# New engine orders, found over several draws of the transposes' landing times, in a linear-attention and gated-MLP block

## The chip, the cores and the metric

The kernel runs on one core of a Trainium2 chip. A core has TensorE (PE) for matmuls, VectorE (DVE), ScalarE (ACT) and GpSimd (POOL) for elementwise work, and SyncE (SP), which here only issues DMAs. Each engine works through its own instructions in order and waits on semaphores for the others. The metric is the device time of one execution in microseconds; the time of a kernel is the median of its runs.

## The reference

One pre-normalised transformer block on x of 2048 tokens by 448 features, in bfloat16: linear attention with 16 heads of 28, then a gated MLP of width 1792, each with a residual.

```python
def _A_ref(x, wqkv, wo):
    B, S, D = x.shape
    H = 16; Dh = D // H
    qkv = (x @ wqkv).reshape(B, S, 3, H, Dh).transpose(2, 0, 3, 1, 4)
    q, k, v = qkv[0], qkv[1], qkv[2]
    phi = lambda t: jnp.where(t > 0, t + 1, jnp.exp(t)) + 1e-6
    pq, pk = phi(q), phi(k)
    kv = jnp.einsum("bhsd,bhse->bhde", pk, v)
    z = jnp.einsum("bhsd->bhd", pk)
    num = jnp.einsum("bhqd,bhde->bhqe", pq, kv)
    den = jnp.einsum("bhqd,bhd->bhq", pq, z)[..., None] + 1e-6
    o = num / den
    return o.transpose(0, 2, 1, 3).reshape(B, S, D) @ wo

h  = x + _A_ref(layernorm(x), wqkv, wo)
h2 = h + (gelu(layernorm(h) @ w_gate) * (layernorm(h) @ w_up)) @ w_down
```

## The kernel before

The 2048 tokens are 16 tiles of 128. The work is a graph of 878 named tasks, and a task is one instruction, one DMA or, on TensorE, a group of matmuls. The number in a name is the tile, or for q the chunk, or for the MLP the block. Each engine has its own written list of task names in ORDERS, and place() puts the tasks of the engine into that order. finalize() and emit() then make semaphores and waits from the dependences: a task waits for the tasks on other engines that wrote what it reads, or still read what it writes. So the lists alone set what stands behind what on an engine, and they can add waits but no wrong result.

The first part goes over all tiles. VectorE takes the statistics (bnst, bnag, lines 462 and 463), ScalarE makes 1/sqrt of the variance (ln, rstd), VectorE or, from tile 4 on, GpSimd normalises (norm, lines 486 and 487). The normalised tile must be turned so that features lie on partitions: tiles 0 to 3 by TensorE (tr, and ev copies the result on ScalarE), the others by a transposing DMA that SyncE issues (xT, line 526), for which ScalarE first doubles the last 64 columns (dup). TensorE then makes k and v of a tile (k, v), ScalarE takes exp (ek) and copies v (evv), GpSimd clamps (cl, line 566), VectorE finishes phi(k) (ph, line 568), and TensorE sums phi(k) times v over the tiles (acc, two halves a and b). In between come the q chunks (qa, qb; eq and rq on ScalarE, cq and pq on GpSimd or VectorE, lines 618, 619 and 627). kz1 and kz2 take the masked sum to SBUF.

The second part goes over pairs of tiles. TensorE makes numerator and denominator (nd, halves a and b), VectorE divides (rd, om, lines 654 and 655), a transposing DMA turns the result (oT, line 729), TensorE multiplies by wo (wo, halves a and b), VectorE adds the residual and takes statistics (hr, line 660; hbnst, hbnag), GpSimd makes 1/sqrt and normalises (hnegm line 481, vpe line 474, pow line 476, normh line 487), VectorE copies the tile to a second place (wrap, line 749), and a transposing DMA turns it (hT, line 750). Tiles 0 and 1 use TensorE for both turns instead (tro, trh; evo, evh).

The MLP goes over chunks of 2, 2, 4, 4 and 4 tiles. A block gu holds the gate and the up product for one slice of the width (28 matmuls of 256 columns in the first two chunks, 14 of 512 after them), ScalarE takes gelu in two halves (ge, line 830), VectorE multiplies (hm, line 832), and down adds up the product with w_down for a pair of tiles (halves a and b) or, for the last four, a tile; out adds the residual (line 756) and dout writes the tile to HBM (line 757).

TensorE's matmuls contract over 64 rows, so one stream works on rows 0 to 63 and one on rows 64 to 127, and they take turns in the program (both()). A half a writes bank P from the first rows and bank Q from the second, its half b the other way round, so b waits for the end of a. PSUM has 8 banks; a gu block uses two of them, and takes the pair that the block two before it used. Almost every matmul comes from line 430 of one helper, the last four down tasks from line 780.

SyncE issues in the order of the fifth list, and each transposing DMA holds it for over a microsecond.

Of the kernel before, what the change touches and what calls it, by code (L numbers as in the profile page):

```python
# [11 lines left out]


ORDERS = (
    "warm0 warm1 tr0 tr1 k0 v0 k1 tr2 v1 tr3 k2 k3 v2 v3 acc0a qa00 acc0b acc1b qb00 k4 acc1a acc2a v4 k5 acc2b acc3b"
    " v5 k6 qa01 v6 qb01 k7 acc3a acc4a v7 acc4b acc5b k8 acc5a acc6a v8 k9 k10 v9 v10 qa10 acc6b acc7b qb10 acc7a k11"
    " acc8a k12 v11 v12 k13 acc8b acc9b v13 acc9a acc10a k14 k15 v14 acc10b acc11b v15 acc11a acc12a acc12b acc13b"
    " qa20 acc13a acc14a qb20 acc14b acc15b acc15a qa11 nd1 nd0 qb11 qa30 nd2a tro1 nd2b qb30 qa21 tro0 qb21 wo1 wo0"
    " qa31 wo2a qb31 wo2b trh0 trh1 nd4a nd4b gu1 gu0 gu3 gu2 wo4a gu5 wo4b gu4 gu7 nd6a nd6b gu6 down0a gu8 wo6a gu9"
    " wo6b down0b nd8a gu11 nd8b gu10 gu13 gu12 down2a wo8a down2b wo8b gu15 nd10a gu14 nd10b gu17 gu16 gu19 gu18 gu21"  # L20
    " wo10a wo10b gu20 nd12a gu23 nd12b gu22 gu25 gu24 gu27 gu26 wo12a down4a wo12b gu28 nd14a gu29 nd14b down4b gu31"
    " gu30 gu33 wo14a gu32 wo14b gu35 gu34 down6a gu36 gu37 down6b gu39 gu38 gu41 gu40 gu43 gu42 gu45 gu44 gu47 gu46"
    " gu49 gu48 gu51 gu50 down8a gu53 down8b gu52 down10a gu55 down10b gu54 down12 down13 down14 down15 down15b",
    "dwk dwv dwk_t tbl ln0 rstd0 ln1 rstd1 ev0 ev1 ln2 ln3 rstd2 rstd3 ek0 evv0 ln4 ev2 rstd4 ev3 ek1 dup4 evv1 dup5"
    " ln6 rstd6 ek2 evv2 evv3 ek3 dup6 dup7 ln8 rstd8 eq0 eq1 dup9 ln12 ek4 rstd12 evv4 ln10 rstd10 ek5 dup8 evv5"
    " dup10 ln14 rstd14 ek6 eq3 evv6 eq2 dup12 dup11 ek7 evv7 ek8 evv8 dup14 dup13 ek9 dup15 evv9 ek10 evv10 eq4 eq5"
    " ek11 evv11 ek12 evv12 evv13 ek13 ek14 evv14 evv15 ek15 eq8 rq8 eq6 rq6 evo1 eq12 evo0 rq10 eq10 rq12 hln1 hrstd1"
    " hln0 hrstd0 eq14 evh0 tbl2 rq14 ge1_0 ge1_1 ge0_1 ge0_0 ge3_1 ge3_0 ge2_1 ge2_0 ge5_1 ge5_0 ge4_1 ge4_0 ge7_1"
    " ge7_0 ge6_0 ge6_1 ge8_0 ge8_1 ge9_1 ge9_0 ge11_1 ge11_0 ge10_0 ge10_1 ge13_1 ge13_0 ge12_0 ge12_1 ge15_0 ge15_1"
    " ge14_0 ge14_1 ge17_0 ge17_1 ge16_0 ge16_1 ge19_0 ge19_1 ge18_0 ge18_1 ge21_0 ge21_1 ge20_0 ge20_1 ge23_1 ge23_0"  # L30
    " ge22_1 ge22_0 ge25_1 ge25_0 ge24_1 ge24_0 ge27_1 ge27_0 ge26_1 ge26_0 ge28_0 ge28_1 ge29_1 ge29_0 ge31_0 ge31_1"
    " ge30_1 ge30_0 ge33_1 ge33_0 ge32_0 ge32_1 ge35_0 ge34_1 ge34_0 ge35_1 ge36_0 ge36_1 ge37_0 ge37_1 ge39_1 ge39_0"
    " ge38_1 ge38_0 ge41_1 ge41_0 ge40_0 ge40_1 ge43_0 ge43_1 ge42_1 ge42_0 ge45_1 ge45_0 ge44_0 ge44_1 ge47_0 ge47_1"
    " ge46_1 ge46_0 ge49_0 ge49_1 ge48_0 ge48_1 ge51_0 ge51_1 ge50_0 ge50_1 ge53_1 ge53_0 ge52_1 ge52_0 ge55_1 ge55_0"
    " ge54_1 ge54_0",
    "wqz pkones bnst0 bnag0 bnst1 bnag1 norm0 v1ones norm1 bnst3 bnst2 bnag3 bnag2 bnst4 bnst5 norm2 bnag4 bnag5"
    " norm3 bnst7 ph0 bnst9 bnst6 bnag7 bnag6 bnst12 ph1 bnst8 bnst11 bnag8 bnag9 ph2 bnst13 bnst10 ph3 bnag13 bnag12"
    " bnag10 bnag11 pq0 pq1 ph4 bnst14 bnst15 bnag14 bnag15 ph5 ph6 pq3 pq2 ph7 ph8 ph9 ph10 pq4 pq5 ph11 ph12 ph13"
    " ph14 ph15 kz2 kz1 rd1 rd0 om1 om0 cq6 rd2 om2 rd3 om3 cq8 pq6 hr1 hbnst1 hr0 hbnag1 hbnst0 hbnag0 normh1 wrap1"
    " normh0 wrap0 hr2 hr3 evh1 hbnst2 rd4 rd5 om4 hbnag2 hbnst3 om5 hm1_0 hm1_1 hbnag3 cq12 cq10 hm0_1 hm0_0 pq10"  # L40
    " cq14 wrap2 pq8 hm3_0 hm3_1 wrap3 pq12 pq14 hm2_1 hm2_0 hm5_1 hr5 hm5_0 hbnst5 hr4 hm4_1 hbnst4 hm4_0 hbnag5"
    " hbnag4 rd6 om6 rd7 om7 hm7_0 hm7_1 hm6_0 wrap4 wrap5 hm6_1 hm8_0 hm8_1 hr6 hm9_0 hbnst6 hm9_1 hr7 hbnag6 hbnst7"
    " hbnag7 out0 out1 rd9 rd8 hm11_1 hm11_0 om8 wrap7 hm10_0 hm10_1 om9 wrap6 hm13_1 hm13_0 hm12_0 hm12_1 out2 hr8"
    " hr9 hbnst8 hbnst9 hm15_1 hm15_0 out3 hbnag8 hbnag9 rd10 hm14_1 hm14_0 rd11 om10 hm17_0 hm17_1 om11 wrap8 wrap9"
    " hm16_0 hm16_1 hm19_0 hm19_1 hm18_0 hm18_1 hm21_0 hm21_1 hr11 hr10 hbnst10 hbnst11 hbnag10 hbnag11 hm20_0 hm20_1"
    " rd13 hm23_1 hm23_0 rd12 om13 hm22_1 hm22_0 om12 wrap10 wrap11 hm25_1 hm25_0 hm24_1 hm24_0 hm27_0 hm26_1 hm27_1"
    " hm26_0 hr12 hr13 hbnst12 hbnst13 hm28_0 hm28_1 hbnag12 hbnag13 rd15 rd14 om15 hm29_1 hm29_0 wrap12 om14 wrap13"
# [865 lines left out]
```

## Time and profile before

| | us |
|---|---|
| median of 3 runs | 198.86 (198.32 to 199.07) |
| the profiled execution | 198.63 |
| its span, first to last instruction | 196.9 |

| engine | busy us | share | instructions |
|---|---|---|---|
| TensorE matmul | 190.9 | 97% | 2192 |
| VectorE | 117.3 | 60% | 301 |
| ScalarE | 78.8 | 40% | 205 |
| GpSimd | 43.4 | 22% | 90 |

A group or timeline row gives the line, the engine, the operation, what it writes and reads, the shape and the count. In a timeline the first two numbers are start and length in microseconds, and a bracket names the idle time before it and what ended it. Two matmul streams run side by side and matmuls overlap their neighbours, so a task's cost is its start to the next task's start, not its length. The chain of waits is followed back from the last instruction: at each step to what released it.

### The profile page before, as it was taken

To read this page: it belongs to the slowest core of one execution; us is meant where nothing else is said; L and a number is where in the kernel's file an instruction comes from. 1 tells how busy PE (TensorE), PEld (TensorE's weight loads), DVE (VectorE), ACT (ScalarE), POOL (GpSimd) and SP (SyncE) were. 2 spreads that over 40 slices of the span, in tenths; PEclk is the share of its full clock that TensorE was granted. 3 is DMA by queue.
4 is the path that set the end of the run, shared out by engine and by line. 5 is a ranking of instruction groups with operands and counts; after the bars stand their busy time and mean duration, and the time that the engine had idled before them with its cause. 6 is when DMAs were issued, how large, how long until landed. Compare 5 with 4: busy or idle time off the path is not lost.

```text
span 196.9 us, 5339 instructions
## 1 busy us (share of the span) xinstructions
PE 190.9 (97%) x2192; PEld 131.2 (67%) x2192; DVE 117.3 (60%) x301; ACT 78.8 (40%) x205; POOL 43.4 (22%) x90
## 2 busy tenths in 40 slices
PE   7899999999899999999999999999999999999994
PEld 7455656553497888998764689955555566777554
DVE  3999636357698955852967845846545554240612
ACT  3799876579672412220342441142214444211100
POOL 3189984300015040500320400500500000000000
DMA  6943466999933243153152160290550000010111
GB/s 195 374 108 70 82 108 156 260 244 214 341 66 63 41 82 68 47 91 62 50 100 50 27 125 0 48 126 23 30 88 27 3 0 0 3 47 3 47 47 47
DMA packets 37256, 17.53 MB, mean 89 GB/s; under 512 B 28272, under 2 KB 36336, under 8 KB 37232
## 3 DMA queue, kind: packets, MB, share of 16 engines
q1 hardware_dynamic: 36352, 16.45, 38.3%
q10 hardware_dynamic: 880, 0.75, 1.2%
q8 instruction: 17, 0.28, 0.6%
q14 instruction: 7, 0.06, 0.1%
HBM read 8.72 MB, written 1.84 MB: 54 GB/s over the span
## 4 chain that ended last, share of the span: by engine, by line
PE 83%; DVE 8%; DMA 4%; POOL 2%; issue 1%; ACT 0%; SPq 0%; DVEq 0%; POOLq 0%
PE ps L430 76%; PE ps L780 5%; DMA oT<-o_sb 2%; DVE st L462 2%; DVE x_sb L660 2%; DMA x_sb<-in_A_x_dram 2%; DVE hh L832 1%; POOL hn L487 1%; DVE o_sb L655 1%; POOL rs L476 1%; DVE x_sb L756 1%; PE ps L495 0%; POOL nm L481 0%; DVE mv L463 0%; DVE pqT L619 0%
## 5 line engine op out<-in xcount | busy, mean ns | idle before, releaser
L430 PE MATMUL ps<-hnT,wgu_sb 64*128 64x512 bf16 (+1 forms) x980 | 90.6, 333 | 0.1
L430 PEld LDWEIGHTS ps<-hnT,wgu_sb 64*128 64x128 bf16 x980 | 61.4, 94 | 22.8 <-DVE hh L832 2.5
L830 ACT ACTIVATE gl<-ps 128x256 bf16<-128x256 f32 x112 | 37.0, 381 | 90.8 <-PE ps L430 74.5
L832 DVE TENSOR_TENSOR hh<-ps,gl 128x256 bf16<-128x256 f32 x112 | 42.5, 418 | 31.5 <-ACT gl L830 31.0
L430 PE MATMUL ps<-wd_sb,hh 64*128 64x448 bf16 x336 | 34.4, 349 | 0.0
L430 PEld LDWEIGHTS ps<-wd_sb,hh 64*128 64x128 bf16 x336 | 25.1, 94 | 6.6 <-DVE x_sb L756 0.2
L430 PE MATMUL ps<-wkv_sb,xnT 64*128 64x448 bf16 x192 | 23.1, 350 | 0.1
L756 DVE TENSOR_TENSOR x_sb<-ps,x_sb 128x448 bf16<-128x448 f32 (+1 forms) x17 | 9.7, 592 | 20.0 <-PE ps L430 13.0
L462 DVE BATCH_NORM_STATS2 st<-x_sb 128x6 f32<-128x448 bf16 x32 | 18.9, 615 | 2.6 <-DMA x_sb<-in_A_x_dram 2.5
L568 DVE SCALAR_TENSOR_TENSOR pk<-ps,tm 128x448 bf16<-128x448 f32 x16 | 9.9, 621 | 9.3 <-POOL tm L566 5.3
L430 PE MATMUL ps<-xnT,wq_sb 64*128 64x512 bf16 x112 | 15.3, 377 | 0.2 <-ACT pqT L616 0.2
L430 PE MATMUL ps<-wo_sb,oT 64*128 64x448 bf16 x98 | 13.2, 349 | 1.0 <-DVE st L462 0.4
L481 POOL TENSOR_SCALAR nm<-mv 128x2 f32<-128x2 f32 x13 | 3.4, 258 | 48.8 <-DVE mv L463 48.4
L430 PEld LDWEIGHTS ps<-wkv_sb,xnT 64*128 64x128 bf16 x192 | 9.0, 94 | 7.5 <-PE ps L430 0.5
L660 DVE TENSOR_TENSOR x_sb<-ps,x_sb 128x448 bf16<-128x448 f32 x16 | 9.5, 617 | 6.5 <-PE ps L430 5.6
L487 POOL TENSOR_SCALAR hn<-x_sb,nm,rs 128x448 bf16<-128x448 bf16 x14 | 11.0, 792 | 0.8 <-POOL rs L476 0.2
L780 PE MATMUL ps<-wd_sb,hh 128*128 128x448 bf16 (+1 forms) x70 | 10.8, 315 | 0.0
L565 ACT ACTIVATE e<-ps 128x448 bf16<-128x448 f32 x16 | 8.7, 545 | 4.5 <-PE ps L430 3.2
L474 POOL TENSOR_SCALAR ln<-mv 128x2 f32<-128x2 f32 x7 | 1.5, 221 | 39.9 <-DVE mv L463 39.7
L566 POOL TENSOR_SCALAR tm<-e 128x448 bf16<-128x448 bf16 x16 | 9.0, 562 | 5.5 <-ACT e L565 5.4
L430 PEld LDWEIGHTS ps<-wo_sb,oT 64*128 64x128 bf16 x98 | 6.6, 94 | 4.9 <-PE ps L430 1.3
L655 DVE TENSOR_TENSOR o_sb<-ps,rd 128x448 bf16<-128x448 f32 x16 | 9.6, 607 | 0.1
(69 smaller groups left out, 145.2 us busy)
## 6 DMA issues: line engine op xcount, KB each, us to landing
out_dram<-x_sb SPq DMA_DIRECT2D x15, 112.0 KB, 1.7
wgu_sb<-in_B_w_gate_dram SPq DMA_DIRECT2D x7, 224.0 KB, 6.7
wgu_sb<-in_B_w_up_dram SPq DMA_DIRECT2D x7, 224.0 KB, 7.3
wd_sb<-in_B_w_down_dram SPq DMA_DIRECT2D x1, 1568.0 KB, 7.2
x_sb<-in_A_x_dram SPq DMA_DIRECT2D x2, 448.0 KB, 5.4
wkv_sb<-in_A_wqkv_dram ACTq DMA_DIRECT2D x2, 336.0 KB, 3.8
x_sb<-in_A_x_dram SPq DMA_DIRECT2D x3, 224.0 KB, 4.4
wo_sb<-in_A_wo_dram SPq DMA_DIRECT2D x2, 336.0 KB, 4.2
```

The source lines that it names most:

```text
L430: ins = e.matmul(o_, l_, r_, start=s_, stop=p_, **kw)
L462: op("dve", lambda e: e.bn_stats(st[:, t, :], src_ap), [b_src], [b_st[t]], "%sbnst%d" % ("" if mv is mv1 else "h", t), 0.53, key, after=after)
L487: return lambda e: e.tensor_scalar(dst, src[:, t, :], nm[:, t:t + 1], rs[:, t:t + 1], ALU.add, ALU.mult)
L565: act_exp(lambda e: e.activation(e1[:, ie, :], oK, AF.Exp), bank(bk), [b_e1[ie]], "ek%d" % t, _c_act(D), kk)
L566: op("pool", lambda e: e.tensor_scalar(tm1[:, ie, :], e1[:, ie, :], 1.0 + EPS, 0.0, ALU.min, ALU.max), [b_e1[ie]], [b_tm1[ie]], "cl%d" % t ...
L568: op("dve", lambda e: e.scalar_tensor_tensor(pk[:, i, :, 0:GW], psK3, EPS, tm1[:, ie, :].rearrange("p (g e) -> p g e", g=NG), ALU.max, ALU ...
L655: op("dve", lambda e: e.tensor_tensor(o_sb[:, so, oc:oc + D].rearrange("p (a e) -> p a e", e=28), nd3[:, :, 0:28], rd[:, i, :].unsqueeze(2 ...
L660: op("dve", lambda e: e.tensor_tensor(h_sb[:, u, :], ps[:, b, 0:D], x_sb[:, u, :], ALU.add), bank(b) + [b_x[u]], [b_h[u]], "hr%d" % u, 0.5 ...
L756: op("dve", lambda e: e.tensor_tensor(x_sb[:, t, c0:c1], ps[:, bk, c0:c1], h_sb[:, t, c0:c1], ALU.add), bank(bk) + [b_h[t]], [bo], "out%d% ...
L780: ins = e.matmul(ps[:, bk, c0:c1], hh[:, j, hsl(t)], wd_sb[:, j, c0:c1], start=(j == 0), stop=(j == NJ - 1))
L830: G.add("act", lambda e, gi=gi, cs_=cs_, psG=psG: e.activation(gl[:, gi, cs_], psG[:, cs_], AF.Gelu_apprx_tanh), r=bank(BK_G[i]), w=[b_glh ...
L832: op("dve", lambda e, dst=dst, srcU=srcU, srcL=srcL: e.tensor_tensor(dst, srcU, srcL, ALU.mult), bank(BK_U[i]) + [b_glh], [b_ar[j_][t % HR ...
```

## The change

Only the five strings of ORDERS are replaced; no task, size or buffer changes. The lists of before came from a search in which every transposing DMA takes one fixed time from issue to landing; the new ones come from a search that scores an order over several draws of these times. 44 of TensorE's 195 places hold another task, 119 of ScalarE's 208, 213 of VectorE's 301, 48 of GpSimd's 86 and 20 of SyncE's 88; most of these by one to three places. The core of it:

```diff
 # TensorE
-warm0 warm1 tr0 tr1 k0 v0 k1 tr2 v1 tr3 k2 k3 v2 v3 acc0a qa00
+warm1 warm0 tr0 tr1 k0 v0 k1 tr2 tr3 v1 k2 acc0a k3 v2 v3 qa00
...
-acc7a k11 acc8a k12 v11 v12 k13 acc8b acc9b v13 acc9a acc10a k14 k15
+acc7a acc8a k11 k12 v11 v12 k13 acc8b acc9b v13 k14 acc9a k15 acc10a
...
-qa11 nd1 nd0 qb11 qa30 nd2a tro1 nd2b qb30 qa21 tro0 qb21 wo1 wo0 qa31 wo2a qb31 wo2b trh0 trh1 nd4a nd4b
+qa11 nd0 nd1 qb11 qa30 nd2a tro0 nd2b qb30 qa21 tro1 qb21 wo1 wo0 qa31 wo2a qb31 wo2b trh1 trh0 nd4a nd4b
-gu1 gu0 gu3 gu2 wo4a gu5 wo4b gu4 gu7 nd6a nd6b gu6 down0a gu8 wo6a gu9
+gu1 gu0 gu3 gu2 gu5 wo4a wo4b gu4 nd6a gu7 nd6b gu6 down0a gu9 wo6a gu8
...
-wo12b gu28 nd14a gu29 nd14b down4b gu31 gu30 gu33 wo14a gu32 wo14b gu35 gu34 down6a gu36 gu37 down6b gu39
+wo12b gu29 nd14a gu28 nd14b gu31 down4b gu30 gu33 gu32 wo14a gu35 wo14b gu34 gu37 gu36 down6a gu39 gu38 gu41 down6b
...
-gu49 gu48 gu51 gu50 down8a gu53 down8b gu52 down10a
+gu49 gu48 down8a gu50 gu51 gu52 down8b gu53 down10a
 # ScalarE
-ln6 rstd6 ek2 evv2 evv3 ek3 dup6 dup7 ln8 rstd8 eq0 eq1 dup9 ln12 ek4 rstd12 evv4 ln10 rstd10 ek5 dup8
+ln6 dup5 rstd6 evv1 ek2 dup6 ln8 ek3 rstd8 evv2 evv3 dup7 eq1 dup8 eq0 dup9 ln12 ek4 ln10 rstd10 rstd12
...
-eq14 evh0 tbl2 rq14 ge1_0 ge1_1
+eq14 evh0 tbl2 ge1_0 ge1_1 rq14
 # VectorE
-kz2 kz1 rd1 rd0 om1 om0 cq6 rd2 om2 rd3 om3 cq8 pq6 hr1
+kz1 kz2 cq8 rd0 rd1 om0 om1 rd2 om2 rd3 cq6 om3 pq8 pq6 cq12 hr1
...
-hr2 hr3 evh1 hbnst2 rd4 rd5 om4 hbnag2 hbnst3 om5 hm1_0 hm1_1 hbnag3 cq12 cq10 hm0_1 hm0_0 pq10 cq14 wrap2 pq8 hm3_0 hm3_1 wrap3 pq12 pq14
+hr2 hr3 evh1 cq14 hbnst2 rd4 hbnst3 rd5 hbnag2 hbnag3 om5 hm1_0 hm1_1 om4 hm0_1 hm0_0 wrap3 wrap2 pq12 hm3_1 hm3_0 pq14 pq10
...
-rd10 hm14_1 hm14_0 rd11 om10 hm17_0 hm17_1 om11
+rd11 rd10 hm14_0 hm14_1 om11 om10 hm17_1 hm17_0
...
-hm28_0 hm28_1 hbnag12 hbnag13 rd15 rd14 om15 hm29_1 hm29_0 wrap12 om14 wrap13 out5 out4 hm31_0 hm31_1 hm30_1 hm30_0
+hm29_0 hbnag13 hm29_1 hbnag12 rd15 rd14 hm28_0 hm28_1 om15 om14 hm31_0 hm31_1 wrap12 out5 wrap13 out4 hm30_0 hm30_1
 # GpSimd
-negm6 norm6 cl2 norm7 negm8 cl3 norm9 cq0 cq1 negm10 cl4 negm12 norm8 norm10 cl5 norm12 norm11 cl6
+negm6 cl1 norm6 norm7 negm8 cl2 cl3 norm8 norm9 cq1 cq0 negm10 negm12 cl4 norm10 norm11 cl5 norm13 norm12 cl6
...
-cl7 norm13 norm14 cl8 norm15 mask_c powwarm cl9
+cl7 norm14 opad2 norm15 cl8 powwarm cl9
 # SyncE
-oT2 oT3 dwd oT4 oT5 hT2 hT3 oT6 oT7 hT5 hT4 dout0 dout1 oT8 oT9 hT7 hT6 dout2 dout3 oT10 oT11 hT8 hT9 oT13 oT12 hT10 hT11
+oT2 oT3 dwd oT5 oT4 hT3 hT2 oT6 oT7 hT5 hT4 dout1 dout0 oT9 oT8 hT6 hT7 dout2 oT11 oT10 hT9 dout3 hT8 oT13 oT12 hT10 hT11
-oT15 hT12 oT14 hT13 dout5 dout4 hT15 hT14
+oT15 oT14 hT12 dout5 hT13 dout4 hT14 hT15
```

90 rows, old and new, of the table ORDERS are left out of this document.

## The prediction

> **What bounds the kernel now.** I read the page first, then the chain of work that ended last, then TensorE's timeline, then VectorE, GpSimd and the DMAs where TensorE stood. On the page, the busy line, the chain's shares and the DMA queues:
>
> ```profile
> PE 190.9 (97%) x2192; PEld 131.2 (67%) x2192; DVE 117.3 (60%) x301; ACT 78.8 (40%) x205; POOL 43.4 (22%) x90
> q8 instruction: 17, 0.28, 0.6%
> PE 83%; DVE 8%; DMA 4%; POOL 2%; issue 1%; ACT 0%; SPq 0%; DVEq 0%; POOLq 0%
> ```
>
> TensorE bounds it: 97% busy, 83% of the chain. The change leaves all 2192 matmuls in the program, so only time can go in which TensorE stands. The chain in order of time names the places (start, length, what):
>
> ```profile
> 59.80 0.96 POOL hn L487
> ...
> 127.61 3.76 DMA oT<-o_sb
> ```
>
> Near 60 the end hung on GpSimd's norm of h, at 127.6 on a transpose of o_sb that was 3.76 us in flight. TensorE's timeline at these places (start, length, out<-in, matmuls):
>
> ```profile
> 54.81 6.30 PE L430 MATMUL ps<-hnT,wgu_sb 64*128 64x256 bf16 x112
> 60.92 1.40 PE L430 MATMUL ps<-wo_sb,oT 64*128 64x448 bf16 x8
> ...
> 68.20 1.74 PE L430 MATMUL ps<-hnT,wgu_sb 64*128 64x256 bf16 x28
> ```
> ```profile
> 126.31 4.85 PE L430 MATMUL ps<-hnT,wgu_sb 64*128 64x512 bf16 x42
> 131.50 0.93 PE L430 MATMUL ps<-wo_sb,oT 64*128 64x448 bf16 x8 [0.34 <-DMA oT<-o_sb]
> 132.26 1.69 PE L430 MATMUL ps<-hnT,wgu_sb 64*128 64x512 bf16 x14
> 133.77 0.75 PE L430 MATMUL ps<-wo_sb,oT 64*128 64x448 bf16 x6
> ```
>
> Lengths overlap, so work is counted from start to start. Four gate/up blocks take 60.92 - 54.81 = 6.11, or 1.53 each; in the later chunks one takes 133.77 - 132.26 = 1.51. So the three blocks from 126.31 should end at 130.84, and wo14a (the 8 matmuls at 131.50) stood 0.66.
>
> **Part 1: gu5, wo4, nd6 (PE order).** From wo4a (60.92) to gu6 (68.20) 7.28 us go by, with three blocks (gu5, gu4, gu7), wo4a, wo4b, nd6a and nd6b in them. The change makes "wo4a gu5 wo4b gu4 gu7 nd6a nd6b" into "gu5 wo4a wo4b gu4 nd6a gu7 nd6b". A b half writes the banks of its a half from the other rows and waits for its end; side by side they pay that. Prices of both forms:
>
> ```profile
> 103.54 1.89 PE L430 MATMUL ps<-wo_sb,oT 64*128 64x448 bf16 x14
> 105.27 1.67 PE L430 MATMUL ps<-hnT,wgu_sb 64*128 64x512 bf16 x14
> ```
> ```profile
> 79.41 0.37 PE L430 MATMUL ps<-kvz,pqT 64*128 64x116 bf16 x7
> 79.61 0.27 PE L430 MATMUL ps<-hnT,wgu_sb 64*128 64x256 bf16 x1
> ```
>
> wo10a and wo10b side by side take 105.27 - 103.54 = 1.73; an nd half with a block behind it 0.20. New sum: 3 x 1.53 + 1.73 + 2 x 0.20 = 6.72, against 7.28: 0.56 less, if nothing new waits. What could wait is gu5, which writes the banks that hm3 reads. VectorE and GpSimd there:
>
> ```profile
> 54.01 0.61 DVE L709 COPY hnT<-ps 128x896 bf16<-128x896 bf16 x1
> 54.54 0.62 DVE L462 BATCH_NORM_STATS2 st<-x_sb 128x6 f32<-128x448 bf16 x1
> ...
> 56.49 0.61 DVE L655 TENSOR_TENSOR o_sb<-ps,rd 128x448 bf16<-128x448 f32 x1
> 57.07 0.76 DVE L832 TENSOR_TENSOR hh<-ps,gl 128x256 bf16<-128x256 f32 x2
> 57.74 0.17 DVE L463 BATCH_NORM_AGGREGATE mv<-st 128x2 f32<-128x6 f32 x1
> ...
> 59.23 0.68 DVE L619 TENSOR_TENSOR pqT<-xn,pqT 112x1024 bf16<-112x1024 bf16 x1
> ```
> ```profile
> 59.80 2.29 POOL L487 TENSOR_SCALAR hn<-x_sb,nm,rs 128x448 bf16<-128x448 bf16 x2
> 68.43 0.22 POOL L474 TENSOR_SCALAR ln<-mv 128x2 f32<-128x2 f32 x1 [6.34 <-DVE mv L463]
> ...
> 69.81 1.42 POOL L487 TENSOR_SCALAR hn<-x_sb,nm,rs 128x448 bf16<-128x448 bf16 x2 [0.18 <-POOL rs L476]
> ```
>
> In VectorE's new order hbnag3 stands ahead of om5, hm1 and om4. After evh1 (54.01) come cq14, two statistics, two short reciprocals and two aggregates, each some 0.08 shorter than its row by overlap; from these rows I work out that hbnag3 ends at 56.5, not 57.91. From the aggregate to the first norm GpSimd takes 69.81 - 68.43 = 1.38, and the two norms take 1.42, or 2.29 where pqT work of VectorE ran beside them. The new order has none of that work beside them, so 56.6 + 1.38 + 1.42 = 59.4 for both. Then wrap3, wrap2, pq12 (0.68) and the two hm3 (0.76) follow: hm3 ends at about 61.0. gu5 comes up at 60.92, and one late stream of a pair is made up within a matmul: 0.1. om4, moved behind hm1 (57.07 + 0.76) with its 0.61, ends at 58.4, so oT4, then the later of the two transposes, lands at 60.9 with the median of 2.5 us that the next part quotes; wo4a now comes up at 62.5 and has room for 4.1. **I take -0.46**; ends: -0.56, and +2.9 if the norms end where they did (62.09; rival 1).
>
> **Part 2: oT14 ahead of hT12 (SP order), and wo14a one block later (PE order).** SyncE's issues there (the length is SyncE's own), the landings of all 14 transposes of o_sb, and the instruction queue in the stretch of 128 to 130 us:
>
> ```profile
> 126.28 1.23 SPq L750 DMA_TRANSPOSE hnT<-hn  x1
> 127.61 2.35 SPq L729 DMA_TRANSPOSE oT<-o_sb  x1
> ```
> ```profile
> DMA to landing us min/median/max: 2.4/2.5/5.1
> ```
> ```profile
> q8 instruction: 1, 0.02, 4.0%
> ```
>
> oT14 was issued at 127.61, behind hT12's issue of 126.28, held SyncE for 2.35 and landed after 3.76 where the median is 2.5. A 16 KB instruction fetch (0.28 MB / 17) fell into that stretch. With hT12 behind it oT14 is issued near 127 (om14 now follows om15 at once, hm28 ahead of both) and lands at 129.5 to 130.8; wo14a comes up at 130.84 + 1.51 = 132.35. Even 5.1 us would land at 132.1. The stall of 0.66 is gone and gu32 fills the place: **-0.66**. Late next is hm30, which gu32 needs: down4b starts a block later, and on VectorE wrap12, out5, wrap13 and out4 stand ahead of hm30, two of them of om's size (0.61) waiting for down4b. From its end two outs, a wrap and hm30 (0.76) take some 2.3, while gu30 and gu33 take 3.0 on TensorE: 0 to +0.2, taken as 0. hT12 and hT13 feed the last chunk, 20 us later.
>
> [...]
>
> **Part 3: the first 40 us.** More norms stand ahead of the clamps on GpSimd, and opad2 ahead of norm15; VectorE's statistics and ACT's copies are shuffled; the two warm-ups are swapped.
>
> ```profile
> 16.00 1.31 PE L430 MATMUL ps<-wkv_sb,xnT 64*128 64x448 bf16 x12
> ...
> 17.33 0.37 PE L430 MATMUL ps<-v,pk 64*128 64x113 bf16 x8
> ```
> ```profile
> 24.01 1.31 PE L430 MATMUL ps<-wkv_sb,xnT 64*128 64x448 bf16 x12
> ...
> 25.58 0.74 PE L430 MATMUL ps<-wkv_sb,xnT 64*128 64x448 bf16 x6
> ```
>
> v8 and k9 took 1.57 where v4 and k5 took 1.33: 0.24 of waiting for xT10. dup8 moves up nine places on ScalarE, so xT8 to xT10 are issued earlier and this goes. Against it, cl2 stands behind one more norm (0.71, half of the 1.42 above), part of which the earlier rstd6 gives back: I estimate 0.25 for ph2, ph3 and k5. The two cancel and I take 0; ends -0.3 (all of the gap, a little more) and +0.5 (most of a norm).
>
> **The rest.** On SP, pairs swap (oT5/oT4, hT3/hT2, oT9/oT8, hT6/hT7, oT11/oT10), dout3 is issued between hT9 and hT8, dout5 and dout4 around hT13; what comes later by an issue of about 1.2 (126.28 above) is read by all of a pair's readers together or a chunk later: 0. om11 ahead of hm17 makes gu19's second stream late by part of an om (0.61): 0 to +0.2, taken +0.1. trh1 ahead of trh0 uses up the slack of evh0 before gu1: 0 to +0.2, taken 0. Splitting "down6a gu36 gu37 down6b" and "down8a gu53" otherwise puts covered blocks between covered blocks, and swaps within a pair (ge, hm, out, dout) move 0.3 inside slack: 0.
>
> **Sum**, against the profiled execution's 198.63 (span 196.9 and 1.73 around it): -0.46 - 0.66 + 0 + 0.1 = -1.0, so 197.6. The median of the runs, 198.86, is 0.23 above that execution; I forecast 197.8 for the new median, 0.5% less, which is about what a measurement of this kernel can tell from no change.
>
> **Rivals.** 1, slower: with wo4a behind it gu5 loses its cover. If GpSimd's norms end at 62.09 as now, wrap, pq12 and hm3 end near 63.9 and TensorE stands 2.9 at gu5 instead of 0.1: about 200.6. It loses from a norm end of 60.4 on. For it: this chain is in the chain of waits now. Against: the 1.4 us by which hbnag3 moves up, and no pqT work beside the norms. 2, no change: late landings are luck, and one falls elsewhere; the 0.66 is not gained in the median: 198.5. For it: landings run from 2.4 to 5.1; against: the fetch comes by instruction count, and the profiled execution is no slower than the others. 3, no change: the early chain (ph2 to ph5, then cl8 behind norm15) keeps the 0.5 of part 3's upper end or two norms' 1.0: 198.3 to 198.8. For it: each clamp now waits behind norms; against: xT10's gap takes it up. 4, more: part 3 gains its 0.3 too: 197.5.
>
> **How the numbers follow.** Forecast 0.46, of which 0.10 falls just short of 0.5%; rival 1 0.16; rival 2 0.18; rival 3 0.14; rival 4 0.06. Faster 0.36 + 0.06 = 0.42, same 0.10 + 0.18 + 0.14 = 0.42, slower 0.16. The forecast's own range is 197.3 to 198.3, its sum with the small ends. The whole range runs from 197.1 (part 3's gain and the good ends too) to 199.3, which takes in rivals 2 and 3 with a run above the median; beyond it lie rival 1 and little else.
>
> **What would show it.** After: wo14a with no DMA named before it; from the first block after nd4 to gu6 0.4 to 0.5 shorter; the norms at 1.4 for two and ended by 59.5; k10 without its gap. Wrong: hm3 past 61.2, or TensorE behind by over 0.3 at the first product with kvz.

## The result, and the profile after

The changed kernel takes 196.57 us (median of 5 runs, 196.28 to 196.70), where the kernel before took 198.44 in 5 runs beside it: a ratio of 0.9896, interval 0.9876 to 0.9916. The forecast was 197.8; the sign was right and the gain was twice the size. The profiled execution took 196.70 (before 198.63) with a span of 194.9 (before 196.9). From the page of the changed kernel, its busy line and the chain's shares:

```profile
PE 190.3 (98%) x2192; PEld 137.9 (71%) x2192; DVE 116.3 (60%) x301; ACT 78.2 (40%) x205; POOL 42.0 (22%) x90
PE 96%; issue 1%; ACT 1%; DVE 1%; POOL 0%; DVEq 0%; ACTq 0%; POOLq 0%
```

TensorE's share of the chain went from 83% to 96%, and the DMAs with their 4% are gone from it: the transpose of 3.76 us, and the first load of x of 3.26, in whose place this chain runs through TensorE's warm-up. I put the start of each TensorE task beside its start in the profile before (after minus before, in us):

| task | what lies ahead of it | difference |
|---|---|---|
| k0 | warm-up, first statistics | +0.52 |
| qa11 | all k, v and acc | +0.29 |
| qa31 | q products, first two nd, wo | +0.33 |
| gu1 | wo2, trh, nd4 | -0.67 |
| gu6 | gu5, wo4, nd6 | -1.31 |
| gu33 | chunks of 2 and 4 tiles | -1.35 |
| gu34 | wo14 | -2.00 |
| down15b | the rest | -1.96 |

Three places make the gain: 1.00 between qa31 and gu1, 0.64 between gu1 and gu6, 0.65 at wo14. The prediction has the last two as its parts 1 and 2. It has no term at all for the first.

Part 1, TensorE's timeline of the changed kernel (start, length, out<-in, count):

```profile
54.13 7.89 PE L430 MATMUL ps<-hnT,wgu_sb 64*128 64x256 bf16 x140
61.77 1.81 PE L430 MATMUL ps<-wo_sb,oT 64*128 64x448 bf16 x14
63.42 1.69 PE L430 MATMUL ps<-hnT,wgu_sb 64*128 64x256 bf16 x28
64.95 0.38 PE L430 MATMUL ps<-kvz,pqT 64*128 64x116 bf16 x8
65.16 1.70 PE L430 MATMUL ps<-hnT,wgu_sb 64*128 64x256 bf16 x28
66.69 0.38 PE L430 MATMUL ps<-kvz,pqT 64*128 64x116 bf16 x8
66.89 1.70 PE L430 MATMUL ps<-hnT,wgu_sb 64*128 64x256 bf16 x28
```

Five blocks (140 matmuls) now run on without a stop, gu5 the last of them; then come wo4a and wo4b side by side (63.42 - 61.77 = 1.65) and two nd halves at 0.21 and 0.20. VectorE and GpSimd of the changed kernel beside it:

```profile
55.53 0.18 DVE L463 BATCH_NORM_AGGREGATE mv<-st 128x2 f32<-128x6 f32 x2
...
59.52 0.75 DVE L832 TENSOR_TENSOR hh<-ps,gl 128x256 bf16<-128x256 f32 x2
```
```profile
57.11 1.41 POOL L487 TENSOR_SCALAR hn<-x_sb,nm,rs 128x448 bf16<-128x448 bf16 x2
```

The aggregates end at 55.71, the two norms at 58.52 after 1.41 us (before: 2.29, to 62.09), and hm3 at 60.27, when gu5 comes up at 60.24.

Part 2, TensorE's timeline, and SyncE's with the landings of oT15 and oT14:

```profile
126.48 4.76 PE L430 MATMUL ps<-hnT,wgu_sb 64*128 64x512 bf16 x42
131.01 0.98 PE L430 MATMUL ps<-wo_sb,oT 64*128 64x448 bf16 x8
131.77 1.74 PE L430 MATMUL ps<-hnT,wgu_sb 64*128 64x512 bf16 x14
133.28 0.79 PE L430 MATMUL ps<-wo_sb,oT 64*128 64x448 bf16 x6
```
```profile
124.38 2.50 SPq L729 DMA_TRANSPOSE oT<-o_sb  x2
127.06 2.15 SPq L750 DMA_TRANSPOSE hnT<-hn  x1
```
```profile
DMA to landing us min/median/max: 2.4/3.2/4.0
```

oT14 was again late (4.0 us, issued at 125.66, landed at 129.65), but wo14a, one block later on TensorE, comes up at 131.01 and names no wait.

The place without a term is wo2a. TensorE's timeline before, and the landing of oT2 and oT3 before:

```profile
48.88 1.04 PE L430 MATMUL ps<-xnT,wq_sb 64*128 64x512 bf16 x8 [0.19 <-ACT pqT L616]
50.29 1.40 PE L430 MATMUL ps<-wo_sb,oT 64*128 64x448 bf16 x8 [0.37 <-DVE st L462]
51.36 0.98 PE L430 MATMUL ps<-xnT,wq_sb 64*128 64x512 bf16 x6
52.00 0.90 PE L430 MATMUL ps<-wo_sb,oT 64*128 64x448 bf16 x6
```
```profile
DMA to landing us min/median/max: 4.2/4.6/5.1
```

And in the changed kernel:

```profile
49.21 1.04 PE L430 MATMUL ps<-xnT,wq_sb 64*128 64x512 bf16 x8 [0.19 <-ACT xn L617]
50.07 0.94 PE L430 MATMUL ps<-wo_sb,oT 64*128 64x448 bf16 x8
50.83 0.83 PE L430 MATMUL ps<-xnT,wq_sb 64*128 64x512 bf16 x6
51.48 0.75 PE L430 MATMUL ps<-wo_sb,oT 64*128 64x448 bf16 x6
```
```profile
DMA to landing us min/median/max: 2.6/3.1/3.5
```

From qa31 to wo2b 3.12 us went by before and 2.27 after. The bracket before names VectorE's statistics, which no wo task depends on; oT2 landed at 50.20 and oT3 at 50.64, and that is what wo2a's two streams waited for. On SyncE's queue both stand behind the 14 transfers of w_gate and w_up (dwg0 to dwu6), the last of which landed at 49.66, and at 48.45 in the changed kernel. Those transfers stand behind the transposes of x, which the new early lists let go sooner (xT8 is issued at 17.12 instead of 19.46, the first transfer of wo at 28.64 instead of 30.36).

### The profile page after: what moved, and what is told of

The parts are those of the page before. It is cut to its first block, busy times and chain, and to the rows that moved or that the text cites. A ratio compares the mean times of both kernels' runs of the same rounds, so it can differ in the third digit from the quotient of the medians.

```text
span 194.9 us, 5336 instructions
## 1 busy us (share of the span) xinstructions
PE 190.3 (98%) x2192; PEld 137.9 (71%) x2192; DVE 116.3 (60%) x301; ACT 78.2 (40%) x205; POOL 42.0 (22%) x90
## 4 chain that ended last, share of the span: by engine, by line
PE 96%; issue 1%; ACT 1%; DVE 1%; POOL 0%; DVEq 0%; ACTq 0%; POOLq 0%
PE ps L430 87%; PE ps L780 6%; PE ps L454 2%; DVE x_sb L660 1%; PE ps L495 1%; ACT xn L617 1%; PE ps L681 0%; ACT xnT L523 0%; PE ps L672 0%; DVE x_sb L756 0%; POOL ones_bf L395 0%; POOL eps_t L398 0%; ACT pqT L616 0%; DVEq L196 0%; ACTq L196 0%
## 5 line engine op out<-in xcount | busy, mean ns | idle before, releaser
L430 PEld LDWEIGHTS ps<-hnT,wgu_sb 64*128 64x128 bf16 x980 | 64.5, 94 | 18.6 <-DVE hh L832 1.7
L430 PEld LDWEIGHTS ps<-wd_sb,hh 64*128 64x128 bf16 x336 | 25.6, 94 | 6.2 <-DVE x_sb L756 0.2
L430 PE MATMUL ps<-wkv_sb,xnT 64*128 64x448 bf16 x192 | 22.4, 350 | 0.4 <-ACT xnT L523 0.4
L430 PEld LDWEIGHTS ps<-wkv_sb,xnT 64*128 64x128 bf16 x192 | 10.1, 94 | 6.3 <-issue 0.8
L430 PE MATMUL ps<-wo_sb,oT 64*128 64x448 bf16 x98 | 12.1, 350 | 0.1
L487 POOL TENSOR_SCALAR hn<-x_sb,nm,rs 128x448 bf16<-128x448 bf16 x14 | 10.0, 720 | 0.8 <-POOL rs L476 0.2
L780 PEld LDWEIGHTS ps<-wd_sb,hh 128*128 128x128 bf16 x70 | 6.7, 98 | 4.3 <-issue 0.4
L570 ACT ACTIVATE v<-ps 128x448 bf16<-128x448 f32 x16 | 8.4, 542 | 2.1 <-PE ps L430 2.1
```

Source lines behind the costliest of these rows:

```text
L430: ins = e.matmul(o_, l_, r_, start=s_, stop=p_, **kw)
L487: return lambda e: e.tensor_scalar(dst, src[:, t, :], nm[:, t:t + 1], rs[:, t:t + 1], ALU.add, ALU.mult)
L780: ins = e.matmul(ps[:, bk, c0:c1], hh[:, j, hsl(t)], wd_sb[:, j, c0:c1], start=(j == 0), stop=(j == NJ - 1))
```

## The experiments

The questions: which lists hold the gain; whether the 1.00 at wo2a is that row of transfers, and why; whether parts 1 and 2 work by the steps of the prediction; and whether late landings are luck. The kernel before was run beside every kernel, and ratios are to those runs.

**The lists cut in two.** Each list is cut at about 40 us, behind acc15a, ek15, ph15, cl15 and dwu6. One kernel has the lists of before ahead of the cut and the new ones behind it:

```diff
 # against the changed kernel, TensorE; the other four engines likewise
-warm1 warm0 tr0 tr1 k0 v0 k1 tr2 tr3 v1 k2 acc0a k3 ...
+warm0 warm1 tr0 tr1 k0 v0 k1 tr2 v1 tr3 k2 k3 v2 v3 acc0a ...
...
 acc15a qa11 nd0 nd1 qb11 qa30
```

> Orders of before up to the last sum over phi(k) v (acc15a, ek15, ph15, cl15, dwu6 on the five engines), orders of after behind it. Theory A, the prediction's: the first 40 us are worth nothing, the whole gain lies behind them; the time is after's, 196.6, so -1.9 against before. Theory B, from the two traces: behind the cut only the pieces at gu4 to gu6 (-0.64) and at wo14a (-0.66) are won, and wo2a waits for oT2 and oT3 as in before; -1.3 against before, 197.1, and no 0.5 us are lost at k0.

Measured: 198.19, ratio 0.9971 (0.9946 to 0.9996). From gu1 to gu34 TensorE gains 1.27, as much as in the changed kernel (1.33). But wo2a starts 0.74 later than before, behind an oT3 that landed at 51.41.

The other has the new lists ahead of the cut and those of before behind it:

```diff
 # against the kernel before, TensorE; the other four engines likewise
-warm0 warm1 tr0 tr1 k0 v0 k1 tr2 v1 tr3 k2 k3 v2 v3 acc0a ...
+warm1 warm0 tr0 tr1 k0 v0 k1 tr2 tr3 v1 k2 acc0a k3 ...
...
 acc15a qa11 nd1 nd0 qb11 qa30
```

> The other half: orders of after up to the same cut, orders of before behind it. Theory A: no change, 198.4 (from -0.3 to +0.5). Theory B: the sums end 0.3 later than in before, but the weights land 1.2 earlier, so oT2 and oT3 land near 49 instead of 50.2 and 50.6, and TensorE saves 1.0 between qa31 and nd4a: -0.7 against before, 197.7, with the waits at wo4a, gu5 and wo14a as in before.

Measured: 197.66, ratio 0.9947 (0.9925 to 0.9969). TensorE is 0.22 behind at acc15a and 0.79 ahead at gu1. The early lists, to which the prediction gave 0, hold about half of the gain, and they pay it out at wo2a, not in the first 40 us.

The changed kernel once more, unedited, beside later runs:

> The changed kernel itself, beside the others on one chip: 196.3 to 196.9, ratio 0.988 to 0.992.

Measured: 196.55, ratio 0.9858 (0.9811 to 0.9905). The two medians, 196.55 and 198.90, give 0.988; the ratio's interval is wide. Its profile has oT3 landed at 49.43 and no wait at wo2a, and TensorE is 0.05 behind the profile before at qa11, not 0.29.

**The warm-up.** The changed kernel with the warm-ups in the order of before:

```diff
-warm1 warm0 tr0 tr1 k0 v0 k1 tr2 tr3
+warm0 warm1 tr0 tr1 k0 v0 k1 tr2 tr3
```

> After with the two warm-ups in before's order (warm0, then warm1), nothing else. Theory B1, the order of the warm-ups sets when TensorE's matmuls get short: they do at 4.6 us as in before instead of past 5.9, k0 starts at 6.9 instead of 7.4; later waits take some of the 0.5 back, so -0.1 to -0.4 against after. Theory B2, the moment at which they get short differs from execution to execution whatever the order: k0's start is not tied to it and the time is after's within 0.1. Theory A: 0.

Measured: 196.52, ratio 0.9897 (0.9861 to 0.9932): no difference. TensorE's warm-up in the profile before, then in this one:

```profile
1.04 3.98 PE L454 MATMUL ps<-ones_bf 128*128 128x128 bf16 x38 [1.04 <-POOL mones L405]
4.96 0.58 PE L430 MATMUL ps<-ones_bf 64*128 64x116 bf16 x16
```
```profile
1.04 4.24 PE L454 MATMUL ps<-ones_bf 128*128 128x128 bf16 x38 [1.04 <-POOL mhalf L401]
5.21 0.75 PE L430 MATMUL ps<-ones_bf 64*128 64x116 bf16 x16
```

The same matmuls in the same order took 4.50 us in one execution and 4.92 in the other. Their spacing falls from 0.107 to 0.056 us at some moment: at 4.64 before, and not within the 38 matmuls here. So the order doesn't set the +0.52 at k0. In 14 of the 16 profiles of this case k0 starts 2.41 to 2.44 us after the second tile of x has landed (4.49 to 4.95); in the first profile of the changed kernel it is 3.00, as the warm-up ran on at the long spacing to 6.17 and the transposes tr0 and tr1 waited for it. The moment varies from one execution to the next: with the first matmul at 1.04 in each, it came at 3.88 in one profile, at 4.64 in the profile before and after 5.85 in that of the changed kernel. What sets it was not shown.

**The MLP weights ahead of oT2 and oT3.** The kernel before, with four of the 14 transfers behind the two transposes (the argument in line 730 that makes place() keep the old order is taken out with it; it makes no wait):

```diff
-dwg4 dwu4 dwg5 dwu5 dwg6 dwu6 oT2 oT3 dwd
+dwg4 dwu4 oT2 oT3 dwg5 dwu5 dwg6 dwu6 dwd
```

> Before, with the last four MLP weight transfers (dwg5, dwu5, dwg6, dwu6) issued behind oT2 and oT3 instead of ahead of them. Theory B, that wo2a waits for transposes which stand behind weights: oT2 and oT3 land by 49, the stop of TensorE from qa31 to wo2b (1.15 us over what after has there) goes, -0.8 to -1.0 against before: 197.5. Theory A, which put no price on this place: 0; a third way is that gu1 then waits for the last weights and gives the gain back.

Measured: 198.74, ratio 1.0008 (0.9986 to 1.0030). oT3 landed at 49.14, wo2a didn't wait and gu1 came 0.77 sooner. Then TensorE stood for the weights themselves:

```profile
54.04 0.82 PE L430 MATMUL ps<-hnT,wgu_sb 64*128 64x256 bf16 x12
55.55 0.28 PE L430 MATMUL ps<-hnT,wgu_sb 64*128 64x256 bf16 x1 [0.69 <-DMA wgu_sb<-in_B_w_gate_dram]
56.28 5.63 PE L430 MATMUL ps<-hnT,wgu_sb 64*128 64x256 bf16 x99 [0.45 <-DMA wgu_sb<-in_B_w_up_dram]
```

The wait was real and was traded for another. Next, the kernel before with the new lists of ScalarE and GpSimd alone, up to ek15 and cl15, which let the transposes of x go early:

```diff
 # GpSimd (ScalarE likewise)
-negm6 norm6 cl2 norm7 negm8 cl3 norm9 cq0 cq1 negm10 cl4 negm12 norm8 norm10
+negm6 cl1 norm6 norm7 negm8 cl2 cl3 norm8 norm9 cq1 cq0 negm10 negm12 cl4 norm10
```

> Before, with ScalarE's and GpSimd's lists of after up to ek15 and cl15 (dup and norm of the tiles 8, 11 and 13 earlier), TensorE, VectorE and SyncE as before. Theory C: the transposes of the normalised tiles are issued 1.4 earlier, so the weights behind them on SyncE land about 1.2 earlier (dwu6 near 48.4 instead of 49.7 to 50.5), oT2 and oT3 with them, and TensorE is 0.7 to 1.0 earlier at gu1 than in before relative to its place at 40 us. Rival C2: the gain needs TensorE's and VectorE's new order too; then dwu6 lands where it did and gu1 does not move. Theory A: nothing moves.

Measured: 199.31, ratio 1.0039 (1.0018 to 1.0060). dwu6 landed at 48.16 and the wait at wo2a is gone, but TensorE is 1.62 late at acc15a; ahead of k4 alone it stands 0.58, ended by the copy of v. The first 40 us keep their length in the changed kernel because VectorE's and TensorE's lists are new there too. I then tried the two steps that seemed to hold the row of transposes, norm8 and norm13 with their dup, in the kernel before:

```diff
-norm9 cq0 cq1 negm10 cl4 negm12 norm8 norm10 cl5 norm12 norm11 cl6 negm14 cq3 cq2 cl7 norm13
+norm8 norm9 cq0 cq1 negm10 cl4 negm12 norm10 cl5 norm12 norm11 norm13 cl6 negm14 cq3 cq2 cl7
-eq0 eq1 dup9 ln12 ek4 rstd12 evv4 ln10 rstd10 ek5 dup8 evv5 ... dup12 dup11 ek7 evv7 ek8 evv8 dup14 dup13
+eq0 eq1 dup8 dup9 ln12 ek4 rstd12 evv4 ln10 rstd10 ek5 evv5 ... dup12 dup11 dup13 ek7 evv7 ek8 evv8 dup14
```

> The lists of before, with two steps alone of the new early order: norm8 ahead of norm9 (GpSimd) with dup8 ahead of dup9 (ScalarE), and norm13 ahead of cl6 with dup13 ahead of ek7. Theory C (the transposes of x are the key: SyncE issues them in order, and dup8 and dup13 hold the row up): xT8 is issued near 17.4 instead of 19.46 and xT15 1.0 to 1.3 earlier, the last MLP weight lands near 48.5 instead of 49.66, oT2 and oT3 near 49.3 instead of 50.2 and 50.6, the gap before k10 goes, and gu1 starts 0.7 to 1.0 earlier against TensorE's place at 40 us; in all -0.5 to -1.0. Theory D (the early chain pays, as it did when both early lists were moved whole): each clamp that comes behind one more norm costs up to 0.7, TensorE is 0.5 to 1.5 behind at acc15a, and the time is that of before or 0.3 to 0.5 longer.

Measured: 199.65, ratio 1.0030 (1.0004 to 1.0056): no gain. xT8 is issued at 17.86, but xT11 then waits until 24.41 (before: 23.36) for dup11, which stands behind eq2 on ScalarE, and eq2 starts 1.16 later than before; xT15 is issued at 30.74, later than before. From there the chain runs as expected, but the other way: the weights land at 51.86, oT2 and oT3 take 5.5 to 6.3, and TensorE waits longer:

```profile
52.45 0.35 PE L430 MATMUL ps<-wo_sb,oT 64*128 64x448 bf16 x1 [1.61 <-DVE hn L486]
52.96 0.91 PE L430 MATMUL ps<-wo_sb,oT 64*128 64x448 bf16 x7 [0.17 <-DMA oT<-o_sb]
```

The opposite edit, in the changed kernel:

```diff
-norm8 norm9 cq1 cq0 negm10 negm12 cl4 norm10 norm11 cl5 norm13 norm12 cl6 negm14 cq3 cq2 cl7 norm14
+norm9 cq1 cq0 negm10 negm12 cl4 norm8 norm10 norm11 cl5 norm12 cl6 negm14 cq3 cq2 cl7 norm13 norm14
-dup8 eq0 dup9 ln12 ek4 ln10 rstd10 rstd12 evv4 ek5 evv5 ... eq3 dup13 eq2 dup12 ek7 evv7 evv8 dup14
+eq0 dup9 ln12 ek4 ln10 rstd10 rstd12 evv4 ek5 dup8 evv5 ... eq3 eq2 dup12 ek7 evv7 evv8 dup13 dup14
```

> The changed kernel, with norm8 and dup8, norm13 and dup13 put back to where before has them. Theory C: xT8 to xT15 are issued 1.0 to 2.0 later again, k10 waits for xT10, the weights land about 1.2 later, wo2a waits for oT3, and TensorE is 0.5 to 1.0 behind the changed kernel from there on: 197.0 to 197.6 where the changed kernel has 196.6. Theory D: the clamps come earlier by a norm, k and acc gain what the transposes lose, and the time is within 0.3 of the changed kernel's.

Measured: 197.37, ratio 0.9920 (0.9891 to 0.9948), some 0.8 longer than the changed kernel, by a way that neither theory had. The weights land 1.03 later, as theory C has it. But norm15, now later, stands ahead of cl8, ph8 comes 0.73 late, and from k11 on TensorE is some 0.7 behind by that; at wo2a it is late enough not to wait. So this run doesn't price the wait.

The price comes from moving one pair of transfers in the kernel before, in the same way, and nothing else:

```diff
-dwg5 dwu5 dwg6 dwu6 oT2 oT3 dwd
+dwg5 dwu5 oT2 oT3 dwg6 dwu6 dwd
```

> The lists of before, with dwg6 and dwu6 alone issued behind oT2 and oT3 instead of ahead of them (two weight transfers, where the run before it moved four). If the wait of wo2a for oT2 and oT3 is what the new early order takes away: oT2 and oT3 land near 49.0 and 49.5 instead of 50.2 and 50.6, dwu6 lands before 53 and gu1 doesn't wait for it; gu1 starts 4.9 to 5.1 behind qa31 where before has 5.9, the time is 0.6 to 1.0 shorter than before's (ratio near 0.996) and the runs lie closer together than before's 3.5. If the wait is made up in any case, or moves to the last weights: gu1 again 5.7 or more behind qa31, or gu2 late, and ratio near 1.000.

Measured: 197.85 against 198.67, ratio 0.9958 (0.9938 to 0.9978), that is 0.82 us. TensorE's timeline of this run and the landing of oT2 and oT3:

```profile
49.02 1.04 PE L430 MATMUL ps<-xnT,wq_sb 64*128 64x512 bf16 x8 [0.19 <-ACT pqT L616]
49.88 0.94 PE L430 MATMUL ps<-wo_sb,oT 64*128 64x448 bf16 x8
50.63 0.83 PE L430 MATMUL ps<-xnT,wq_sb 64*128 64x512 bf16 x6
51.28 0.75 PE L430 MATMUL ps<-wo_sb,oT 64*128 64x448 bf16 x6
```
```profile
DMA to landing us min/median/max: 2.5/2.8/3.1
```

No wait: qa31 to wo2b takes 2.26, and gu1 doesn't wait for dwu6 (landed at 52.33). The runs also lie closer together: 197.54 to 198.34 (12 runs), against 197.79 to 199.62 (17 runs) for the kernel before. With 12 runs each, two kernels that keep this row of before spread over 2.05 and 1.76 (the early lists of before with the later new ones, and part 2 alone further down), and the new early lists with the later ones of before over 0.85. In six profiles that keep the early lists of before and the weights ahead of oT2, qa31 to wo2b took 3.12, 3.41, 3.66, 3.18, 3.31 and 2.27; the wait is thus 0 to 1.4 in an execution, 0.9 in the mean. In four with the new early lists and nothing else moved there it was 2.27 three times and 2.74 once. The last weight landed at 48.77 to 50.67 in the six (48.77 in the one without a wait) and at 48.10 to 49.16 in the four.

The same edit in the changed kernel:

> The changed kernel with the same edit. Where the wait is gone already, nothing is left to gain but what some executions still wait (0.5 in one profile): 196.3 to 196.6 where the changed kernel has 196.55.

Measured: 196.56, ratio 0.9897 (0.9867 to 0.9927), the changed kernel's own time: nothing of this wait was left to gain. No kernel here is clear of the changed one.

**Part 1 on TensorE alone.** The kernel before, with one edit:

```diff
-gu2 wo4a gu5 wo4b gu4 gu7 nd6a nd6b gu6
+gu2 gu5 wo4a wo4b gu4 nd6a gu7 nd6b gu6
```

> Before, with TensorE's order of after in one place: gu5 wo4a wo4b gu4 nd6a gu7 nd6b for wo4a gu5 wo4b gu4 gu7 nd6a nd6b; VectorE as before. The prediction's rival 1 on its own ground: hm3 still stands behind the norms of tiles 2 and 3 on GpSimd and ends near 62.3, so gu5, which comes up at 60.9, stands 1.4; from gu2 to gu6 the piece takes 0.8 to 0.9 longer than in before instead of 0.6 shorter, about +0.8 us. If VectorE's order had nothing to do with it, the piece gets 0.5 to 0.6 shorter here too.

Measured: 200.39, ratio 1.0094 (1.0060 to 1.0127). TensorE and GpSimd of this run:

```profile
63.02 1.70 PE L430 MATMUL ps<-hnT,wgu_sb 64*128 64x256 bf16 x27 [1.20 <-DVE hh L832]
64.45 1.82 PE L430 MATMUL ps<-wo_sb,oT 64*128 64x448 bf16 x14
66.11 1.69 PE L430 MATMUL ps<-hnT,wgu_sb 64*128 64x256 bf16 x28
68.39 0.38 PE L430 MATMUL ps<-kvz,pqT 64*128 64x116 bf16 x8 [0.58 <-DVE x_sb L660]
```
```profile
60.43 2.29 POOL L487 TENSOR_SCALAR hn<-x_sb,nm,rs 128x448 bf16<-128x448 bf16 x2
```

With VectorE's list of before the norms take 2.29 and end at 62.72, gu5 waits for hm3 and nd6a for hr4, and TensorE loses 1.51 from gu2 to gu6. So TensorE's new order is a loss with the lists of before on the other engines. That it is VectorE's list which makes it a gain is read from the two profiles (the aggregates end sooner, and no pqT work stands beside the norms); VectorE's list was not run alone.

**Part 2 on TensorE alone, and complete.** First only TensorE's slot, SyncE and VectorE as before:

```diff
-gu33 wo14a gu32 wo14b gu35
+gu33 gu32 wo14a gu35 wo14b
```

> Before, with wo14a one block later on TensorE (gu33 gu32 wo14a gu35 wo14b) and SyncE's list as before, so oT14 is still issued behind hT12. If the later slot is enough: oT14 lands near 131.4 and wo14a comes up near 132.3, no wait, -0.6 at gu34. If the issue order is needed: wo14a still waits.

Measured: 200.02, ratio 1.0061 (1.0030 to 1.0091). TensorE and VectorE:

```profile
135.66 0.38 PE L430 MATMUL ps<-hnT,wgu_sb 64*128 64x512 bf16 x1
137.03 1.68 PE L430 MATMUL ps<-hnT,wgu_sb 64*128 64x512 bf16 x13 [0.99 <-DVE hh L832]
```
```profile
136.02 0.62 DVE L660 TENSOR_TENSOR x_sb<-ps,x_sb 128x448 bf16<-128x448 f32 x1 [1.99 <-PE ps L430]
136.56 0.41 DVE L832 TENSOR_TENSOR hh<-ps,gl 128x256 bf16<-128x256 f32 x1
```

The wait ahead of wo14a is gone (0.65 gained to gu34), although oT14 wasn't issued sooner. But hr14 (136.02) waits for wo14b, which is a block later, and hm32_1 stands behind hr14: gu34's second stream waits, and 1.19 is lost again by gu36. Then with SyncE's swap and VectorE's hr14 moved back:

```diff
 # besides TensorE's edit above
-oT15 hT12 oT14 hT13
+oT15 oT14 hT12 hT13
-om15 hm29_1 hm29_0 wrap12 om14 wrap13
+hm29_1 hm29_0 om15 om14 wrap12 wrap13
-hm32_0 hr14 hm32_1 hr15 hbnst15 hm35_0 hbnst14 ...
+hm32_0 hm32_1 hm35_0 hm35_1 hr14 hbnst14 ...
-ge35_0 ge34_1 ge34_0 ge35_1
+ge35_0 ge35_1 ge34_1 ge34_0
```

> The lists of before, with part 2 alone and complete: oT14 ahead of hT12 on SyncE, wo14a and wo14b one block later on TensorE, and on VectorE hr14 behind hm32_1, hm35_0 and hm35_1 (ge35_1 ahead of ge34 on ScalarE). If VectorE's list was what gave the gain back in the run with TensorE's slot alone: no wait before wo14a, none at gu34, and TensorE 0.65 ahead from gu33 to gu36 and to the end, ratio near 0.997. If a later place pays in any case (down6a, gu37): 0.65 ahead at gu34 and less than 0.3 at the end, ratio near 1.000.

Measured: 198.51, ratio 0.9981 (0.9956 to 1.0007).

```profile
131.53 1.07 PE L430 MATMUL ps<-wo_sb,oT 64*128 64x448 bf16 x8
...
134.37 1.83 PE L430 MATMUL ps<-hnT,wgu_sb 64*128 64x512 bf16 x14
```

No wait is left at wo14a or gu34; TensorE gains 0.65 against the profile before from gu33 to gu34 and gives 0.13 of it back by the end. By time the gain is 0.4 with an interval that reaches no change. The 0.65 is the price in the one profile of the kernel before: in seven profiles with TensorE's program and wo14a's place of before, gu33 to gu34 took 6.22 to 6.65, and with the later slot it takes 5.86 to 5.88, so the wait is worth 0.5 in the mean. SyncE's swap was not run by itself; with the slot alone oT14 landed at 131.68, 1.15 ahead of wo14a.

**Late landings.** The kernel before with TensorE's program 27 instructions shorter (38 warm-up matmuls of 128 columns become 9 of 512 and 2 of 128; nothing reads their results):

```diff
-                for _ in range(n):
-                    ins = e.matmul(ps[:, 0, 0:128], ones_bf[:], ones_bf[:], start=True, stop=True)
+                for _ in range(9):
+                    ins = e.matmul(ps[:, 0, 0:512], ones_bf[:], ones_bf[:].unsqueeze(1).to_broadcast([128, 4, 128]), start=True, stop=True)
+                for _ in range(2):
+                    ins = e.matmul(ps[:, 0, 0:128], ones_bf[:], ones_bf[:], start=True, stop=True)
```

> Before with its orders, and the 38 warm-up matmuls of 128 columns replaced by 9 of 512 and 2 of 128, which take as long but are 27 fewer in TensorE's program; the warm-up's results are not used. Theory F, that a transpose lands late when a 16 KB block of TensorE's instructions is fetched while it is in flight: each fetch now comes 27 matmuls later in the stream, 1.5 to 3 us; oT5, hT4, hT11, hT12 and oT14, which were late by 1.3 to 1.9, land in 2.4 to 3.0, others become late in their place, and the stop of 0.66 ahead of wo14a goes. Rival: these transposes are late for their place among the DMAs, and stay late.

Measured: 199.35, ratio 1.0028 (1.0001 to 1.0054). The landings of oT15 and oT14, and TensorE there and at k8:

```profile
DMA to landing us min/median/max: 2.4/2.4/2.5
```
```profile
24.01 0.74 PE L430 MATMUL ps<-wkv_sb,xnT 64*128 64x448 bf16 x6 [0.34 <-DMA xnT<-xn]
...
131.98 1.07 PE L430 MATMUL ps<-wo_sb,oT 64*128 64x448 bf16 x8
```

oT14 lands after 2.46 instead of 3.76, hT11 after 3.35 instead of 4.92, hT14 after 2.93 instead of 5.10, and wo14a doesn't wait, with all orders as before. Others are late instead: xT8 after 3.87 (2.43) and xT9 after 4.27 (2.47), for which k8 waits. In this profile TensorE gains 0.65 at wo14a and is still 0.61 behind the profile before at the end, 0.43 of it since k0. The instruction blocks come at other moments in this run (133.07 instead of 128.24 beside wo14a), and the late transposes went with them. Without this edit hT11 lands after 4.7 to 5.0 in all nine profiles with the later lists of before; with the new ones it was 4.4 to 4.6 in four and 2.9 in two. Counted over all 16 profiles, oT2 and oT3 aside: of 306 transposes with no instruction fetch under way none took more than 3.1 us, and of 148 in which the fetch of a 16 KB block began at least 0.2 us ahead of the landing, 139 took more than 3.2, up to 5.5.

## Why the prediction was right or wrong

**Part 1** was right in its mechanism and small by 0.18. Taken -0.46, measured -0.64. The wo4 pair took 1.65 where the wo10 pair had given 1.73, and gu5's late stream, taken at 0.1, cost nothing that shows. The aggregates ended 0.8 sooner than worked out (55.71 for 56.5), but 0.7 of this is the gain ahead of gu1, by which evh1 and gu5 come sooner too. Rival 1's mechanism is real: with TensorE's order alone the norms end at 62.72 and 1.51 is lost (its 2.9 was worked out for VectorE's new order, in which pq12 stands ahead of hm3).

**Part 2** was right: taken -0.66, measured -0.65, and the step that does it is the later slot on TensorE. oT14 was late again, yet landed at 129.65, within the 129.5 to 130.8 of the prediction. That the size fits so well is in part luck: both numbers use the same profile of the kernel before, and over seven profiles the wait was worth 0.5 in the mean. Late next was not hm30, as the prediction had it, but hm32_1 behind hr14, as the run with TensorE's slot alone shows; the new list of VectorE puts hr14 behind it.

**Part 3** was taken at 0 with ends -0.3 and +0.5, and in the two profiles compared the first 40 us cost 0.29. The gap before k10 went, as it said: k6 starts 0.60 later than before, k10 only 0.12 later. Against it stood 0.52 at k0, which the prediction did not look for; the run with the warm-ups exchanged shows that this varies from one execution to the next and isn't set by their order. qa11 starts at 40.06 to 40.41 in five profiles with the new early lists (one with the warm-ups of before) and at 40.13 to 40.56 in seven with those of before, so 0 was a fair price for these 40 us.

**The step that failed** is the end of part 3: it followed the earlier transposes of x only as far as k10, and gave everything between 40 us and gu1 no term but trh's 0. They also move everything behind them on SyncE's queue, the 14 weight transfers and then oT2 and oT3, for which wo2a waited. That was worth 1.00 in the two profiles compared, and 0.82 in the median where that wait alone was taken out. A bracket of 0.37 that named VectorE's statistics stood at wo2a in the timeline; the landing row of 4.2 to 5.1 us for oT2 and oT3, and the 3.12 from qa31 to wo2b against 2.27 of the work itself, would have told what it was. With this term the sum of -1.0 would have been -1.8 to -2.0, against the -1.96 measured. That it closes so well is in part luck: in this pair of profiles the 0.29 lost in the first 40 us stands against the 0.18 of part 1 and the 0.1 of gu19.

**The rest**: +0.1 was taken for gu19 and nothing came (gu6 to gu33 -0.04). **Rival 2** (late landings are luck) fell in the main: they mostly repeat with the order, and move when TensorE's instruction count moves. The fetch beside oT14 began behind 1594 matmuls in the profile before (at 128.24) and behind 1592 in that of the changed kernel (at 126.66). A transpose that was in flight when a block was fetched did pay here: oT14 landed after 3.76 us where the median is 2.5, 1.3 more. **Rival 3** (the early chain keeps a norm's time) shows up where only ScalarE's and GpSimd's lists are new (1.62 at acc15a), not in the change as a whole. **Rival 4** had the sign of the miss, but put it in the first 40 us.

## What to carry to other kernels

When a step moves a DMA, follow its queue to the end: the first reader of what stands last on it may be the one that gains. Where a stretch takes longer than its work and the bracket names work that it doesn't read, look at when the DMAs landed that feed it. A new order on one engine can be a loss by itself and a gain with the orders of its neighbours, so price it with theirs.

## What was not expected of the hardware

A transpose of 2.4 to 2.5 us (2.9 to 3.1 for h) mostly takes 3.2 to 5.5 when a 16 KB instruction block is fetched while it is in flight (139 of 148). That these blocks are TensorE's follows from the run with fewer matmuls, where they came at other moments (133.07 instead of 128.24 beside wo14a); which transposes they meet mostly repeats with the order (hT11 landed after 4.7 to 5.0 in all nine profiles with the later lists of before). The wait for oT2 and oT3 came out between 0 and 1.4 us with the same early lists: the row of 14 weight transfers took 15.2 us from first issue to last landing where there was no wait, and 15.8 to 16.7 in the five profiles with one. The runs of the kernel before spread over 1.8 us; with the wait taken out they spread over 0.8. The two norms on GpSimd took 2.29 us with pqT work of VectorE beside them and 1.41 without.
